# Attention and a low-rank token-mixing MLP in one kernel: another order for the first batch, split fp32r matmuls for t, one PSUM pool

## The chip, the cores and the metric

The kernel runs on one core of one Trainium2 chip. The metric is device time in microseconds (us). The kernel before takes 1001.5 us, the median of three runs (1000.41 to 1001.79). One further execution was recorded by the profiler, and every row of the profile comes from that one.

## The reference

For each of 8 batches, 8 heads, 576 tokens and 64 values per head (q, k and v are inputs in float32):

```python
scores = (q @ k.T) / sqrt(64)
mask_plain = (rel >= 0) & (rel < 32)                       # heads 0 to 3; rel = query position - key position
mask_dil = (rel >= 0) & (rel < 128) & (rel % 4 == 0)       # heads 4 to 7
scores = where(mask, scores, -1e9); scores -= scores.max(-1)
attn = exp(scores); attn /= attn.sum(-1) + 1e-9
x = (attn @ v) as [batch, token, 512]
h = x.T @ U @ V              # per batch, U is [576, 32], V is [32, 576]
u = x + h.T
out = u + relu(u @ w1) @ w2  # w1 is [512, 2048], w2 is [2048, 512]
```

Below, t = Uᵀx is the [32, 512] product of a batch, and the mix is Vᵀt, which is added to x.

## The kernel before

**Precision.** The large matmuls run in fp32r, a form of float32 that keeps fewer bits. To keep the precision, an operand is split into a high part (an fp32r copy) and a low part (what the copy lost), and a product is the sum of three matmuls: high by high, low by high, high by low. A plain fp32 matmul is one instruction in the program and, in the profile, about four times as long as an fp32r one of the same columns (five of 256 columns take 2.51 us, four fp32r ones 0.48 us).

**Attention.** A batch's 18 token tiles of 64 (nine plain, nine dilated) make nine *groups* of two tiles and four units. Groups 0 to 8 are batch 0, 9 to 17 batch 1, and so on to 71. A group's work is: `scores` (32 matmuls, L305), `soft_add` (mask, VectorE, L316), `soft_top` (row maximum, VectorE, L324), the subtraction and exp (GpSimd and ScalarE, L334; from group 9 on four exps on ScalarE, L336), the turn of p into `pts` (TensorE for groups 0 to 17, L342; from group 18 on 16 transposes on VectorE, L358), two steps later `products` (L376), then `weighted` (sums and reciprocal on VectorE, L389 and L390, and the normalisation into x, L416; for groups 0 to 5 the normalisation is eight scaled copies on ScalarE). The dilated half is written to DRAM rows (L428) and fetched back in token order (L433).

**Batch 0** is a loop of its own, steps s = 0 to 10: scores(s), turn_pe(s - 1), products(s - 2), and at the end of a step what lists by engine (`todo`) and the load list name for it: V's unpacking and copies (`pick_v`, L614, which copies V into the four bands of 32 partitions of `vs`), U's unpacking, t of batch 0 (`t_first`, L466), x laid out transposed in PSUM (`lay_x`) with the mix added by matmul (`lay_mix`) and split (`split_sums`, L532), and the unpacking of the first weight pieces (`PRE` gives piece and step). Weights come from DRAM as words that ScalarE, VectorE and GpSimd unpack into high and low parts, one piece for each hidden block and layer (L183, L187, L247).

**The MLP** takes the 36 tiles of 128 tokens in chunks: chunk 0 has four tiles, chunk 1 two, and ten chunks have three. A chunk has 16 hidden blocks, each with twelve first-layer matmuls (ph, L838), the hidden activation hh on ScalarE (L843), its low part hl on VectorE (L844), and for each tile three second-layer matmuls (acc, L857), one hidden block behind.

**The order of the rest.** Instructions stand in each engine's queue in the order in which the program writes them; no scheduler moves them. Between the matmuls of the MLP the program calls `slot()`, seven times a hidden block in chunk 0, five times in chunk 1 and six times later. A queue of side work is sorted by number, and each slot takes out what is due. `STEP_AT` gives the slots of the groups' bursts (`burst`: products of group g - 2 and scores of g); all other numbers follow from these: `split_x` (x into high and low, ScalarE L448 and GpSimd L449), `t_mm` (t by matmul, L476 for batch 1 in fp32, L481 from batch 2 on in fp32r), `t_evict` (t out of PSUM: ScalarE copies, L492, a subtraction on VectorE), `mix` (L501) and `mix_add` (onto x, VectorE, L507), and the transposes that lay out the next chunk (L586 splits them).

**PSUM** has eight banks. Batch 0 uses a pool "first" (ph 2, ps 3, acc 3). Then come a pool with ps 2 and ph 2 and beside it four acc banks in chunk 0, and three acc banks and one mixing bank ("ms", for t and the mix) from chunk 1 on. Closing a pool makes the next one's users wait for the last users of the closed one.

## Time and profile before

| | |
|---|---|
| median of three runs | 1001.5 us |
| profiled execution | 1001.12 us, of which the span is 999.3 us |
| TensorE (PE) busy | 952.0 us |
| VectorE (DVE) busy | 593.6 us |
| ScalarE (ACT) busy | 289.9 us |
| GpSimd (POOL) busy | 89.3 us |
| first weight matmul | at 47.03 us |
| granted clock of TensorE | 0.991 in the mean |

The page names engines PE, PEld (TensorE's weight loads), DVE, ACT, POOL and SP (the queue that issues most DMAs). L838 is line 838 of the kernel. A group's row reads: line, engine, operation, output <- inputs, shapes, count, then busy time and mean duration in ns, then the engine's idle time before it and what ended it. "fp32r" marks an engine's output; the profile writes fp32r operands of matmuls as f32.

### The profile page before, as it was taken

The page shows a single profiled execution, that of the slowest core. Times are in us where ns is not written, and L with a number is a line of the kernel's source. Part 1 is how long each engine was busy: PE and PEld are TensorE (multiplying, and loading weights), DVE is VectorE, ACT ScalarE, POOL GpSimd, SP SyncE. Part 2 cuts the span into 40 slices and gives each one's busy share as a digit, 9 for nine tenths or more (in the row PEclk, how much of TensorE's full clock was granted, in tenths as well). Part 3 has the DMA queues.
Part 4 walks back from the last instruction along what each step waited for, and adds up shares of the span by engine and source line. Part 5 has one row for each costly group of instructions (what it writes and reads, how often), then busy time and mean ns, then how long its engine had stood idle before and what let it go on. Part 6 is the DMA issues. An engine that isn't in the chain of part 4 may idle for free.

```text
span 999.3 us, 22345 instructions
## 1 busy us (share of the span) xinstructions
PE 952.0 (95%) x9000; PEld 812.1 (81%) x9000; DVE 593.6 (59%) x1942; ACT 289.9 (29%) x772; POOL 89.3 (9%) x114
## 2 busy tenths in 40 slices
PE   6799989998999899999899999999999999999998
PEld 4577757787888778888788888888788888999997
DVE  4478776776678667667656766765766753211211
ACT  4577852222222222122222222222321311111110
POOL 3122221000100110010000110010100100000000
PEclk9999998999999999999999999999999999999999
DMA  7467841352143223232323312323214201201000
GB/s 261 165 221 241 258 127 43 90 161 67 48 129 110 65 68 100 87 97 64 106 66 105 102 50 77 109 80 102 79 41 136 81 15 28 66 22 43 32 1 32
DMA packets 79144, 94.30 MB, mean 94 GB/s; under 512 B 8256, under 2 KB 57536, under 8 KB 79040
## 3 DMA queue, kind: packets, MB, share of 16 engines
q1 hardware_dynamic: 79040, 92.86, 30.0%
q8 instruction: 71, 1.16, 0.5%
q14 instruction: 33, 0.27, 0.1%
HBM read 70.81 MB, written 22.02 MB: 93 GB/s over the span
## 4 chain that ended last, share of the span: by engine, by line
PE 70%; DVE 12%; issue 7%; ACT 6%; DMA 2%; SPq 1%; POOL 1%; POOLq 0%; ACTq 0%; DVEq 0%
PE ph L838 32%; PE acc L857 29%; DVE pt L358 2%; PE att L305 2%; PE att L376 2%; ACT hh L843 1%; ACT p L336 1%; DVE vw L187 1%; PE m L501 1%; DVE x L866 1%; PE t L481 1%; POOL xhl L449 1%; DVE hl L844 1%; DVE sign L183 1%; DVE x L416 1%
## 5 line engine op out<-in xcount | busy, mean ns | idle before, releaser
L844 DVE SCALAR_TENSOR_TENSOR hl<-ph,hh 128x384 fp32r<-128x384 f32 (+2 forms) x192 | 106.9, 557 | 302.2 <-ACT hh L843 301.1
L857 PE MATMUL acc<-w2h,hh 128*128 128x512 f32 x576 | 230.5, 400 | 0.0
L857 PE MATMUL acc<-w2h,hl 128*128 128x512 f32 x576 | 227.9, 396 | 1.5 <-DVE hl L844 1.4
L857 PE MATMUL acc<-w2l,hh 128*128 128x512 f32 x576 | 227.6, 395 | 0.9 <-POOL w2l L247 0.9
L843 ACT ACTIVATE hh<-ph 128x384 fp32r<-128x384 f32 (+2 forms) x192 | 93.9, 489 | 463.4 <-PE ph L838 461.8
L358 DVE STREAM_TRANSPOSE pt<-p 32x64 f32<-32x64 f32 x864 | 203.8, 236 | 28.4 <-ACT p L336 14.8
L838 PE MATMUL ph<-uth,w1h 128*128 128x384 f32 (+2 forms) x768 | 168.3, 341 | 3.5 <-ACT uth L586 2.2
L838 PE MATMUL ph<-uth,w1l 128*128 128x384 f32 (+2 forms) x768 | 168.0, 341 | 0.0
L838 PE MATMUL ph<-utl,w1h 128*128 128x384 f32 (+2 forms) x768 | 167.8, 340 | 0.0
L838 PEld LDWEIGHTS ph<-uth,w1h 128*128 128x128 f32 x768 | 136.4, 189 | 20.1 <-ACT uth L586 3.1
L838 PEld LDWEIGHTS ph<-uth,w1l 128*128 128x128 f32 x768 | 133.5, 189 | 4.3 <-issue 0.6
L838 PEld LDWEIGHTS ph<-utl,w1h 128*128 128x128 f32 x768 | 133.4, 189 | 3.7
L857 PEld LDWEIGHTS acc<-w2h,hl 128*128 128x128 f32 x576 | 108.3, 188 | 27.9 <-DVE hl L844 2.6
L857 PEld LDWEIGHTS acc<-w2h,hh 128*128 128x128 f32 x576 | 108.7, 189 | 19.3 <-issue 0.8
L857 PEld LDWEIGHTS acc<-w2l,hh 128*128 128x128 f32 x576 | 108.7, 189 | 17.1 <-POOL w2l L247 1.2
L336 ACT ACTIVATE p<-p,top 128x64 f32<-128x64 f32 x252 | 69.0, 338 | 156.8 <-DVE top L324 156.6
L449 POOL TENSOR_TENSOR xhl<-x,xhl 128x256 fp32r<-128x256 f32 (+1 forms) x60 | 44.7, 755 | 609.9 <-ACT xhl L448 356.2
L305 PE MATMUL att<-qk 64*32 64x64 f32 x2304 | 43.9, 238 | 6.4 <-DMA qk<-qk 5.7
L305 PEld LDWEIGHTS att<-qk 64*32 64x32 f32 x2304 | 35.0, 111 | 11.3 <-DMA qk<-qk 6.2
L316 DVE SCALAR_TENSOR_TENSOR p<-att,mask_sb 128x128 f32<-128x128 f32 x144 | 34.4, 279 | 13.2 <-PE att L305 13.0
L376 PEld LDWEIGHTS att<-v,pt 64*32 64x32 f32 x2016 | 18.8, 106 | 17.6 <-issue 14.0
L501 PE MATMUL m<-ts,vs 128*128 128x256 f32 x66 | 21.2, 321 | 12.3 <-ACT ts L492 7.1
(95 smaller groups left out, 622.8 us busy)
## 6 DMA issues: line engine op xcount, KB each, us to landing
qk<-qk SPq DMA_DIRECT2D x64, 288.0 KB, 3.5
v<-vv SPq DMA_DIRECT2D x126, 130.0 KB, 3.3
...
```

What stands on the lines that cost most here:

```text
L183: nc.vector.scalar_tensor_tensor(out=s32[:, cs], in0=lo, scalar=29, in1=s32[:, cs], op0=ALU.logical_shift_right, op1=ALU.bitwise_or)
L305: nc.tensor.matmul(att[h][r * WIN:(r + 1) * WIN, u * KB:(u + 1) * KB], lhsT=q_, rhs=k_, start=True, stop=True, tile_position=(h * D, r * WIN))
L316: nc.vector.scalar_tensor_tensor(out=p_sb[:, h], in0=att[h][:, 0:2 * KB].rearrange("p (u k) -> p u k", k=KB), scalar=1.0 / 8.0, in1=m, op0 ...
L336: nc.scalar.activation(out=p4[:, n], in_=p4[:, n], func=AF.Exp, bias=top[:, n:n + 1])
L358: nc.vector.transpose(out=pts[g % 2][ks, :, rs], in_=p_sb[rs, :, u, WIN * k:WIN * (k + 1)])
L376: nc.tensor.matmul(att[u][row:row + WIN, o:o + DV], lhsT=pt[us_, h, WIN * r:WIN * (r + 1)], rhs=loaded[g, 1][r // 2][us_, r % 2, h * DV:(h ...
L449: nc.gpsimd.tensor_tensor(out=xhl[rs, 1], in0=x[rs], in1=xhl[rs, 0].bitcast(F32), op=ALU.subtract)
L501: nc.tensor.matmul(mixed[b, i, c], lhsT=vs[:, o:o + P], rhs=t_sb[b, c], start=True, stop=True)
L838: nc.tensor.matmul(ph, lhsT=w[:, k, :], rhs=u[:, k, :], start=(n == 0 and m == 0), stop=(n == 2 and m == KC - 1))
L843: nc.scalar.activation(out=hh, in_=ph, func=AF.Relu)
L844: nc.vector.scalar_tensor_tensor(out=hl, in0=ph, scalar=0.0, in1=hh.bitcast(F32), op0=ALU.max, op1=ALU.subtract)
L857: nc.tensor.matmul(acc[i], lhsT=h[:, ss], rhs=w, start=(c > 1 and f == 1 and n == 0), stop=(f == FC and n == 2))
```

## The change

Nine edits come together.

1. `STEP_AT`: groups 17 and 18 have their bursts at slots 81 and 114 (before, groups 19 and 20 at 95 and 114). The products of groups 16 and 17 have bursts of their own (`LAST`, slots 90.6 and 94.1), without scores.
2. One PSUM pool for the whole program: ps 2, ph 2, acc 4. t from batch 2 on and the mix use the acc banks.
3. Batch 0: all loads are issued first, the first weight piece behind them, and the first two pieces are unpacked in other steps (`PRE`).
4. V's four copies are made by eight split fp32r matmuls in steps 6 and 7 (before: four fp32 matmuls in step 3), through ph banks, with the picking matrices and V split beforehand.
5. t of batch 0 is made by split fp32r matmuls from x split on ScalarE and GpSimd (`split_first`), but for the one part `t_first(3, 0)`, which stays fp32. t of batch 1 is made as in later batches, by `split_x` and two fp32r matmuls a part.
6. U's stationary matrix has 128 columns for each part: three copies of the high part and the low part. So t comes out of PSUM in four bands.
7. `t_evict` is one ScalarE copy of 128 partitions and one VectorE subtraction on 32 of them (before: a copy, a subtraction and one or two further copies).
8. The normalisation of groups 0 to 5 moves from ScalarE to VectorE.
9. The high and the low halves of `split_sums` are issued apart; t starts five slots behind the splits (before four, or nine behind the first); the mix comes four slots behind the eviction's number.

```diff
-PRE = [(0, 6), (1, 10)]
+PRE = [(0, 8), (1, 9)]
-NX = 17
+NX = 16
-STEP_AT = [(NGB, 2), (2 * NGB + 1, 95), (2 * NGB + 2, 114), (3 * NGB + 1, 232), (4 * NGB + 1, 342), (NG + 1, 914)]
+STEP_AT = [(NGB, 2), (2 * NGB - 1, 81), (2 * NGB, 114), (3 * NGB + 1, 232), (4 * NGB + 1, 342), (NG + 1, 914)]
...
-    first = first_open.enter_context(tc.tile_pool(name="first", bufs=3, space=bass.MemoryType.PSUM))
+    psum = ctx.enter_context(tc.tile_pool(name="psum", bufs=2, space=bass.MemoryType.PSUM))
-    us = const.tile([P, 9, 2 * RANK], F32R, name="us")
+    us = const.tile([P, 9, 4, RANK], F32R, name="us")
...
-                if g < 6:
+                if g < 0:
                     for h in range(2):
                         nc.scalar.activation(out=o[:, h], in_=pv[rs, h, 0:D], func=AF.Copy, scale=ssum[rs, u, h:h + 1])
...
+        pool, tag, n_ = (work, "z", ZS) if b == 1 and i < 2 else (xpool, "x", NX)
+        xhl = pool.tile([P, 2, HALF_D], F32R, tag=tag, name=f"xhl{b}_{i}_{c}", bufs=n_)
...
+    def split_first(i, c):
...
+        nc.scalar.copy(out=xhl[rs, 0], in_=m[rs])
+        xs[0, i, c] = xhl
+        rest[i, c] = lambda: nc.gpsimd.tensor_tensor(out=xhl[rs, 1], in0=m[rs], in1=xhl[rs, 0].bitcast(F32), op=ALU.subtract)
...
     def t_first(i, c):
...
-        nc.tensor.matmul(t_ps[0, c], lhsT=u32[rs, k * RANK:(k + 2) * RANK], rhs=m[rs],
-                         start=new, stop=(i == (0 if c else len(DPART) - 2)), skip_group_check=True)
+        xhl = xs.pop((0, i, c))
+        for k in range(2):
+            nc.tensor.matmul(t_ps[0, c], lhsT=u, rhs=xhl[:, k], start=(new and k == 0), stop=(last and k == 1),
+                             skip_group_check=True)
...
     def t_evict(b, c):
-        nc.scalar.copy(out=ts_[r[0]], in_=tp[r[0]])
-        nc.vector.tensor_tensor(out=ts_[r[1]], in0=tp[r[0]], in1=ts_[r[0]].bitcast(F32), op=ALU.subtract)
-        if b > 0:
-            nc.scalar.copy(out=ts_[r[2]], in_=tp[r[1]])
-        nc.scalar.copy(out=ts_[r[3]], in_=tp[r[0]])
+        nc.scalar.copy(out=ts_, in_=tp)
+        nc.vector.tensor_tensor(out=ts_[lo], in0=tp[lo], in1=ts_[lo].bitcast(F32), op=ALU.subtract)
...
-        mixed[b, i, c] = accs.tile([P, HALF_D], F32, tag="ms", name=f"m{b}_{i}_{c}", bufs=1)
+        mixed[b, i, c] = psum.tile([P, HALF_D], F32, tag="acc", name=f"m{b}_{i}_{c}", bufs=4)
...
-    loads = {0: [lambda: load_qk(5), lambda: load_v(4)], 1: [lambda: load_qk(6), lambda: load_v(5)],
-             2: [lambda: load_qk(7), lambda: load_v(6)], 3: [lambda: load_qk(8), lambda: load_v(7), lambda: w_fetch(0)],
-             4: [lambda: load_v(8), lambda: w_fetch(1)], 5: [lambda: w_fetch(2)], 6: [lambda: w_fetch(3)],
...
+    for g in range(4, NGB):
+        load_qk(g)
+        load_v(g - 1)
+    load_v(NGB - 1)
+    w_fetch(0)
+    loads = {3: [lambda: w_fetch(1)], 5: [lambda: w_fetch(2)], 7: [lambda: w_fetch(3)], 8: [lambda: w_fetch(4)],
...
+    def pick_v(i):
+        vps[i] = psum.tile([P, 2, VC], F32, tag="ph", name=f"vps{i}", bufs=2)
+        for k in range(2):
+            for m in range(2):
+                nc.tensor.matmul(vps[i][:, k], lhsT=picks[:, m, 2 * i + k].rearrange("p i r -> p (i r)"), rhs=vhl[:, m],
+                                 start=(k == 0 and m == 0), stop=(k == 1 and m == 1), skip_group_check=True)
+    def keep_v(i):
+        nc.scalar.copy(out=vs[:, 2 * i * VC:2 * (i + 1) * VC], in_=vps.pop(i).rearrange("p k c -> p (k c)"))
...
+    LAST = [step_at(2 * NGB - 1) + 9.6, step_at(2 * NGB - 1) + 13.1]
+    for i, at_ in enumerate(LAST):
+        g = 2 * NGB - LAG + i
+        add(step_at(2 * NGB - 1) + 1 + i, take_v, g)
+        add(at_, burst, -1, g)
+        add(at_ + 1, after_burst, -1, g)
...
-            at_ = max([end_1 if c == 0 else 0] + splits) + (5 if c == 0 else 9)
             if b == 1:
-                at_ = step_at(2 * NGB + c * -1 + 1) + 3
+                at_i = [LAST[0] - 4 + 1.2 * i for i in range(n)] if c else [LAST[0] + 2.5 + 0.6 * i for i in range(n - 2)] + [LAST[1] + 1.5, LAST[1] + 2]
+                at_t = [LAST[1] + 2.5 + 0.3 * i for i in range(n)] if c else [LAST[1] + 4.5 + 0.3 * i for i in range(n)]
+            else:
+                at_i = [splits[i] + i if c else max(splits[0:i + 1] + [end_1]) + 0.02 * i for i in range(n)]
+                at_t = [a + 5 for a in at_i]
+            at_ = at_t[-1] + 0.3
+            m_at = FIRST + 4 + 12 * (1 - c) if b == 1 else at_ + 4
```

Three places show how the order moves. The first is the queue of SP in batch 0, from the values of group 5 to the first weight piece (raw0). qk and v are a group's loads, xd0 the rows of the dilated half that are written to DRAM. Before:

```order
L282 DMA v5_187<-vv 128x520
L428 DMA xd0_246<-xp0_241 128x256
L270 DMA qk7_250<-qk 128x576
L282 DMA v6_252<-vv 128x520
L428 DMA xd0_246<-xp1_316 128x256
L270 DMA qk8_322<-qk 128x576
L282 DMA v7_324<-vv 128x520
L221 DMA raw0_326<-w1 128x4x256
```

With the change:

```order
L280 DMA v5_131<-vv 128x520
L268 DMA qk7_133<-qk 128x576
L280 DMA v6_135<-vv 128x520
L268 DMA qk8_137<-qk 128x576
L280 DMA v7_139<-vv 128x520
L280 DMA v8_141<-vv 128x520
L219 DMA raw0_143<-w1 128x4x256
L425 DMA xd0_254<-xp0_251 128x256
```

All loads of batch 0 and the first weight piece now stand ahead of the first write of dilated rows.

The second is TensorE at the end of batch 1, in hidden block 14 of chunk 0 (t1_0 and t1_1 are the two halves of t of batch 1, att the banks of scores and products). Before:

```order
L305 MATMUL att19_1_2074<-qk19_1757 32x64 x4
L838 MATMUL ph0_14_2107<-uth0_698,w1h_13_1876 128x512 x4
L838 MATMUL ph0_14_2107<-uth0_698,w1l_13_1877 128x512 x4
L838 MATMUL ph0_14_2107<-utl0_699,w1h_13_1876 128x512 x4
L476 MATMUL t1_0_2150<-x4_506,us_73 64x256
L476 MATMUL t1_0_2150<-x5_1591,us_73 64x256
L476 MATMUL t1_0_2150<-x6_1593,us_73 64x256
L476 MATMUL t1_0_2150<-x7_1595,us_73 64x256
L476 MATMUL t1_0_2150<-x8_1561,us_73 64x256
L857 MATMUL acc0_0_800<-w2h_13_1878,hh0_13_2020 128x512
```

With the change:

```order
L494 MATMUL t1_1_2106<-xhl1_0_1_1940,us_73 128x256 x2
L494 MATMUL t1_1_2106<-xhl1_1_1_1952,us_73 128x256 x2
L872 MATMUL ph0_14_2083<-utl0_756,w1h_13_1892 128x512 x4
L494 MATMUL t1_1_2106<-xhl1_2_1_1968,us_73 128x256 x2
L494 MATMUL t1_1_2106<-xhl1_3_1_1990,us_73 128x256 x2
L494 MATMUL t1_1_2106<-xhl1_4_1_2016,us_73 128x256 x2
L891 MATMUL acc0_0_822<-w2h_13_1894,hh0_13_1986 128x512
L891 MATMUL acc0_0_822<-w2l_13_1895,hh0_13_1986 128x512
L891 MATMUL acc0_0_822<-w2h_13_1894,hl0_13_1987 128x512
L494 MATMUL t1_0_2136<-xhl1_0_0_2043,us_73 128x256 x2
L494 MATMUL t1_0_2136<-xhl1_1_0_2047,us_73 128x256 x2
```

The scores of group 19 are no longer there, both halves of t stand between the pieces of the MLP, and each part is two matmuls on a split of x.

The third is VectorE at the same place, around the normalisation of group 17, the last of batch 1 (ssum17, x7 and x8; vw and sign are a weight piece's unpacking, p18 and p19 belong to groups 18 and 19 of batch 2). Before:

```order
L358 STREAM_TRANSPOSE pt0_79<-p18_1966 32x2x32 x2
L187 SCALAR_TENSOR_TENSOR vw29_2033<-vw29_2033,sign1_76 128x512
L358 STREAM_TRANSPOSE pt0_79<-p18_1966 32x2x32 x2
L389 TENSOR_SCALAR ssum17_2114<-att19_0_2073 128x2
L389 TENSOR_SCALAR ssum17_2114<-att19_1_2074 128x2
L390 RECIPROCAL ssum17_2114<-ssum17_2114 128x4
L416 TENSOR_TENSOR x7_1595<-att19_0_2073,ssum17_2114 64x128
L416 TENSOR_TENSOR x7_1595<-att19_1_2074,ssum17_2114 64x128
L416 TENSOR_TENSOR x8_1561<-att19_0_2073,ssum17_2114 64x128
L416 TENSOR_TENSOR x8_1561<-att19_1_2074,ssum17_2114 64x128
L316 SCALAR_TENSOR_TENSOR p19_2122<-att19_0_2073,mask_sb_71 128x128
```

With the change:

```order
L181 SCALAR_TENSOR_TENSOR sign1_76<-raw29_0_1978,sign1_76 128x256
L181 SCALAR_TENSOR_TENSOR sign1_76<-raw29_1_1979,sign1_76 128x256
L185 SCALAR_TENSOR_TENSOR vw29_2027<-vw29_2027,sign1_76 128x512
L386 TENSOR_SCALAR ssum17_2088<-att17_0_2056 128x2
L386 TENSOR_SCALAR ssum17_2088<-att17_1_2057 128x2
L387 RECIPROCAL ssum17_2088<-ssum17_2088 128x4
L413 TENSOR_TENSOR x7_1644<-att17_0_2056,ssum17_2088 64x128
L413 TENSOR_TENSOR x7_1644<-att17_1_2057,ssum17_2088 64x128
L413 TENSOR_TENSOR x8_1615<-att17_0_2056,ssum17_2088 64x128
L413 TENSOR_TENSOR x8_1615<-att17_1_2057,ssum17_2088 64x128
```

The transposes of group 18 and the mask of group 19 no longer stand around the normalisation.

249 lines of the change are left out of this document (125 added, 124 removed).

## The prediction

> **What bounds the kernel now.** I read the page first, then TensorE's waits in three stretches, then the order of time around the two places where they gather. The page:
>
> ```profile
> span 999.3 us, 22345 instructions
> PE 952.0 (95%) x9000; PEld 812.1 (81%) x9000; DVE 593.6 (59%) x1942; ACT 289.9 (29%) x772; POOL 89.3 (9%) x114
> ```
>
> TensorE is busy for 952 of 999.3 us, so an edit counts where TensorE idles, runs slowly or does work it need not do. The idle 47 us lie in three places. The first is the attention of batch 0, before the first weight matmul (columns: start, duration, instructions, idle time before and what ended it):
>
> ```profile
> 10.37 0.68 PE L305 MATMUL att<-qk 64*32 64x64 f32 x32 [0.18 <-DMA qk<-qk]
> 12.12 2.69 PE L614 MATMUL vps<-vn,pick 128*128 128x176 f32 x8
> 18.81 0.68 PE L305 MATMUL att<-qk 64*32 64x64 f32 x32
> 20.63 0.68 PE L305 MATMUL att<-qk 64*32 64x64 f32 x32
> 28.06 0.69 PE L342 MATMUL ptp<-id_sb,p 128*128 128x128 f32 x2 [2.05 <-ACT p L334]
> 28.68 1.97 PE L466 MATMUL t<-xp,u 128*64 128x256 f32 x4
> 33.98 0.46 PE L376 MATMUL pv<-v,pt 64*32 64x65 f32 x32
> 35.35 1.08 PE L466 MATMUL t<-x,u 128*64 128x256 f32 x4 [0.53 <-ACT t L492]
> 47.03 2.01 PE L838 MATMUL ph<-uth,w1h 128*128 128x512 f32 x4 [1.24 <-DVE utl L532]
> 20.33 6.07 DMA raw<-w
> ```
>
> The L305 rows are the scores of groups 3, 5 and 6; an undisturbed step takes 20.63 - 18.81 = 1.82 us. From group 3's scores to step 9 (33.98) are six steps and 23.6 us. What stretches them is V's copies (2.69 us), the t matmuls (1.97 us for two calls), and the exp behind the last row, which is of the chain of waits: ScalarE had the first weight piece, still in flight, ahead of the exp in its queue.
>
> The second place is the end of batch 1 (window rows: stretch, length, busy time of PE, PEld, DVE, ACT and POOL, granted clock, DMA):
>
> ```profile
> 135.37 2.51 PE L476 MATMUL t<-x,us 64*64 64x256 f32 x10
> 149.83 4.68 PE L476 MATMUL t<-x,us 64*64 64x256 f32 x10 [3.32 <-DVE p L316]
> 148.49 1.00 DVE L416 TENSOR_TENSOR x<-att,ssum 64x128 f32<-64x128 f32 x4
> 148.00:150.00 2.00, 0.17 (x1) 0.20 (x2) 1.86 (x10) 0.18 (x1) 0.00 (x0) 0.88 0.02 5
> 150.00:152.00 2.00, 2.00 (x5) 0.83 (x5) 1.49 (x6) 1.10 (x4) 0.00 (x0) 0.50 0.00 0
> 156.00:158.00 2.00, 2.00 (x10) 1.59 (x9) 0.83 (x3) 1.98 (x6) 1.15 (x1) 0.91 0.00 0
> ```
>
> TensorE idles 3.32 us because VectorE, full in that stretch, normalises the last group of batch 1 only at 148.49; then the clock is granted at half for about 6 us (three such rows from 150 to 156, the first shown), and the same ten t instructions take 4.68 us instead of 2.51.
>
> The third place is the short waits in batches 2 to 7 (TensorE's waits, window 250 to the end: total, times, longest):
>
> ```profile
> PE m L501 <- ACT ts L492: 6.0, 4, 2.8
> PE t L481 <- POOL xhl L449: 3.4, 8, 0.5
> PE t L481 <- ACT xhl L448: 3.0, 4, 1.3
> PE m L501 <- DVE x L507: 2.9, 6, 1.3
> ```
>
> **The change, part by part.** (a) The prelude. As many bytes as before lie ahead of group 3's keys, so its scores stay near 10.4. The weight piece is now fetched behind all of batch 0 but used only in step 8, so the wait for it goes, and V's copies leave step 3. The normalisation of groups 0 to 5 moves from ScalarE to VectorE, which I take as what paces the steps (groups of VectorE, 10 to 34 us; the L416 row from 170 to 226):
>
> ```profile
> L324 DVE TENSOR_REDUCE top<-p 128x4 f32<-128x256 f32 x7 | 2.9, 420 | 0.7
> L316 DVE SCALAR_TENSOR_TENSOR p<-att,mask_sb 128x128 f32<-128x128 f32 x12 | 2.9, 282 | 5.1 <-PE att L305 5.0
> L389 DVE TENSOR_SCALAR ssum<-pv 128x2 f32<-128x2 f32 x14 | 1.5, 149 | 0.0
> L390 DVE RECIPROCAL ssum<-ssum 128x4 f32<-128x4 f32 x7 | 1.2, 177 | 0.2
> L183 DVE SCALAR_TENSOR_TENSOR sign<-rawu,sign 128x448 int32<-128x448 int32 x1 | 1.0, 1002 | 0.0
> L187 DVE SCALAR_TENSOR_TENSOR u<-u,sign 128x448 int32<-128x448 int32 x1 | 0.6, 625 | 0.0
> L416 DVE TENSOR_TENSOR xp<-att,ssum 128x128 f32<-128x128 f32 (+1 forms) x10 | 2.4, 286 | 0.2
> ```
>
> One step: 2 x 0.282 + 0.420 + 2 x 0.149 + 0.177 + 2 x 0.286 = 2.0 us. Six steps are 12.2; U's unpacking adds 1.6, V's about 0.7 (176 columns of 448, with a floor), group 4's second half 0.6: 15.1. In TensorE's queue between one step's turn and the next scores now stand V's eight split matmuls and six t passes. From 1.97 us for two fp32 calls of four passes each a pass of 256 columns costs 0.25 at that speed: 1.5 for t, 1.4 for V, and up to 1 us until ScalarE has copied V out of the one bank that the second half and t0 share. Half of this lies beside VectorE's work; I charge 1.5. Step 9 comes at 10.4 + 16.6 = 27.0 instead of 34.0: 7 us. Behind step 9 stood 13.0 us; the wait of 1.24 us for all subtractions should mostly go with the pool's closing, but GpSimd now has five to seven subtractions in series ahead of the last t. I credit 0.5. Sum (a): 7.5 us, between 3 and 10.
>
> (b) The end of batch 1. Ten fp32 t calls become 20 passes; two rows show the pace of 256 columns at full clock:
>
> ```profile
> 199.37 0.64 PE L838 MATMUL ph<-uth,w1h 128*128 128x256 f32 x4
> 199.85 0.64 PE L838 MATMUL ph<-uth,w1l 128*128 128x256 f32 x4
> ```
>
> Four take 0.48 us, so 20 take 2.4, against 2.51 + 4.68/2 = 4.85 at full clock: 2.4 saved. The last products now come without scores, in slots 90.6 and 94.1, and group 18's scores only in slot 114, so the transposes of groups 18 and 19 no longer stand ahead of the normalisation on VectorE. If the idle 3.32 us goes, so does the half clock (0.12 x 2 + 0.5 x 6 + 0.09 x 2 = 3.4 us lost). Together 9.1. New there are ten splits:
>
> ```profile
> L449 POOL TENSOR_TENSOR xhl<-x,xhl 128x256 fp32r<-128x256 f32 x48 | 35.6, 755 | 358.9 <-ACT xhl L448 277.8 <-issue 23.4 <-PE ph L838 19.2
> L448 ACT CAST xhl<-x x60: 387/402/409, 220.2 to 828.3; 128x256 fp32r<-128x256 f32 x48, 64x256 fp32r<-64x256 f32 x12
> 120.00:146.00 26.00, 24.93 (x286) 18.17 (x285) 20.28 (x54) 18.50 (x52) 6.59 (x5) 1.00 0.51 158
> L336 ACT ACTIVATE p<-p,top 128x64 f32<-128x64 f32 x12 | 3.5, 337 | 8.2 <-DVE top L324 8.2
> ```
>
> ScalarE (18.5 of 26 us busy) gets 10 x 0.40 = 4.0 us and loses the eight exps of groups 18 and 19 (2.7 us) and four of six t copies; GpSimd (6.6 of 26) gets 7.6 us. Is the last split in time? Count from T, the end of the 14th ph, by estimates from the rows. TensorE has two product bursts (1.0), seven second-layer blocks of three (7 x 0.7 = 4.9, by 2.08 us for nine, quoted in (c)), one ph (2.8) and seven t parts (1.7) ahead of it: T + 10. On the other side ScalarE runs one hidden activation, two splits and a piece's four copies (7 x 0.4 = 2.8), VectorE unpacks and normalises (2.6), ScalarE copies (two pieces' rest and two splits, 1.6), GpSimd subtracts twice (1.5): T + 8.5. Behind it in ScalarE's queue stand the hidden activations, behind those the second layer. I charge 1.1. Sum (b): 8, between 2 and 9.
>
> (c) Batches 2 to 7. In the program's count a three-tile chunk has six slots per hidden block, and these rows of the chain of waits give the slot's length:
>
> ```profile
> 247.52 2.10 PE ph L838 x12
> 260.08 2.08 PE acc L857 x9
> ```
>
> (2.10 + 2.08)/6 = 0.70 us. Split to t grows from four slots to five, against waits of 0.5 us (GpSimd) and at most 1.3 (ScalarE): of 6.4 us I leave 2.0, with 0.5 in it because batch 2's five splits now fall together. The eviction loses two copies and their queueing behind VectorE, and the mix moves a slot away: of 6.0 I leave 2.0. The 2.9 for the one mixing bank stay. That is 8.4; since waits move when everything before them moves, I take 7, between 3 and 10.
>
> (d) The price. By the program's numbers groups 18 to 28 come every 118/10 = 11.8 slots instead of 118/8 = 14.75 (from group 20 on), most of them in chunk 1:
>
> ```profile
> 170.00:226.00 56.00, 53.77 (x691) 47.19 (x690) 42.72 (x163) 12.32 (x40) 2.18 (x3) 1.00 0.44 131
> L358 DVE STREAM_TRANSPOSE pt<-p 32x64 f32<-32x64 f32 x87 | 20.5, 236 | 1.4
> PE m L501 <- DVE x L507: 2.2, 3, 1.5
> ```
>
> 1.3 more groups in chunk 1, each 16 x 0.236 + 2.0 = 5.8 us, raise VectorE from 42.7 to about 50 of 56 us (90%). Against some 2 us of late hl stand the 2.2 us of mixing waits (the last row, window 47 to 250), which fall away since chunk 1 holds two of the four acc banks. Net 0, between -4 and +2. Keeping one PSUM pool costs no instruction; t's wider stationary side (128 columns instead of 64) costs nothing, since the ph rows above hold their pace with 128.
>
> Sum: 7.5 + 8 + 7 + 0 = 22.5 us. The profiled execution took 1001.12 us, 0.4 below the median of the runs and 1.8 above its span: 978.6, with the median 979.
>
> **The rivals.** *The prelude stays slow.* TensorE's batch 0 speed doubled only within its dense stretch (two t calls: 1.97 us at 28.68, 1.08 at 35.35). The change thins that stretch. If the array is still slow for the 32 fp32 instructions that lay x out, then at about 0.125 us more each (2.50 us for 20 fast ones) 4 us go and (a) is 3.5: 983. Against it: those instructions are dense themselves. The Trainium skill, "TensorE: Matmul & The Clock Gate", Part 1, says that the array runs at half clock by default, goes to full after about 3.4 us of sustained activity and falls back after an idle window of that length; the fall after 3.32 us idle agrees. By that rule it is this rival that the thinner prelude gets, with 983. The window rows of the prelude grant 1.00 throughout, so there only durations can tell.
>
> *The wait at the end of batch 1 comes back in another form.* ScalarE's queue holds weight unpacking, splits and hidden activations in one order; if it is 3 us behind, TensorE waits for GpSimd's last split and the clock falls again: (b) keeps the 2.4 us of passes and little else: 985.
>
> *The waits of batches 2 to 7 only move.* (c) gives 0 to 1: 985.5.
>
> *Slower.* VectorE at 90% in chunk 1 cannot keep the step of 11.8 slots; a group's transposes finish later than its products, TensorE waits 3 us and falls to half clock. One such gap costs 3.3 + 3.4 = 6.7 us by the rows at 148 to 158. It decides from the fourth gap in chunk 1 and the first third of chunk 2: 978.6 + 26.8 = 1005. For it speaks the in-order queue; against it that two steps lie between scores and products, and that VectorE at 42.7 of 56 us made TensorE idle only 2.2 us.
>
> **How the numbers follow.** Forecast 0.56 (own range 972 to 984), slow prelude 0.14 (983), returned wait 0.13 (985), moved waits 0.12 (985.5), slower 0.03 (1005); 0.02 for a mix that ends level. Two of the middle rivals together give 990. The upper ends of (a) to (d) give 31 us and 970. The range is 969 to 991. Under 0.2% (2 us) cannot be told from no change; faster by more: 0.95, same 0.02, slower 0.03.
>
> **What would show it.** The first weight matmul should start between 37 and 41 us, not 47.0 (slow prelude: 42 to 44, with lay-out matmuls at 0.25 us). The half clock near 150 should be gone and t of batch 1 should take about 2.4 us of TensorE in all. The sum of the four waits from 250 on should be 6 to 9 us instead of 15.3. VectorE should show about 90% in chunk 1 with hl as a wait of under 3 us. A first weight matmul after 44, or a half clock anywhere behind 60 us, would make the prediction wrong.

## The result and the profile after

The changed kernel takes 982.78 us, the median of four runs (982.27 to 982.89), against 1000.95 us for the kernel before in the same session. The ratio is 0.982, 95% interval 0.9803 to 0.9837: faster by 18 us. The forecast was 979, with a range of 969 to 991. The page of its profiled execution (982.7 us) begins:

```profile
span 980.8 us, 22338 instructions
PE 942.0 (96%) x9000; PEld 815.3 (83%) x9000; DVE 600.0 (61%) x1953; ACT 281.1 (29%) x735; POOL 109.3 (11%) x139
```

TensorE is busy 10 us less and idle 8.5 us less. To see where, both spans are cut at the same places of the program: where the hidden activation of the first block starts (end of the prelude), of the 17th (start of chunk 1), of the 49th (start of chunk 3) and of the 192nd, the last. Window rows of the kernel before (stretch, length, busy time of PE, PEld, DVE, ACT, POOL, granted clock, DMA share, GB/s):

```profile
0.00:52.56 52.56, 38.42 (x717) 25.50 (x718) 24.68 (x83) 26.77 (x77) 11.60 (x22) 0.97 0.62 208
52.56:173.44 120.88, 114.38 (x1131) 86.62 (x1130) 89.81 (x218) 77.40 (x186) 27.10 (x20) 0.97 0.56 179
173.44:312.11 138.67, 131.73 (x1436) 114.43 (x1435) 100.15 (x370) 35.02 (x106) 8.83 (x13) 1.00 0.32 95
312.11:991.30 679.19, 663.31 (x5705) 582.58 (x5704) 376.35 (x1269) 150.24 (x403) 41.77 (x59) 0.99 0.23 70
```

And of the changed kernel:

```profile
0.00:46.02 46.02, 35.10 (x718) 27.49 (x719) 26.54 (x94) 24.68 (x59) 21.02 (x35) 1.00 0.71 238
46.02:162.50 116.48, 107.51 (x1034) 84.12 (x1033) 84.53 (x183) 77.74 (x185) 37.67 (x32) 1.00 0.56 180
162.50:305.49 142.99, 135.81 (x1532) 117.42 (x1531) 109.24 (x404) 35.38 (x110) 8.75 (x13) 0.99 0.32 98
305.49:972.81 667.32, 659.44 (x5705) 583.26 (x5704) 377.08 (x1269) 142.85 (x384) 41.84 (x59) 1.00 0.24 71
```

| stage | before | after | difference |
|---|---|---|---|
| prelude | 52.56 | 46.02 | -6.5 |
| chunk 0 | 120.88 | 116.48 | -4.4 |
| chunks 1 and 2 | 138.67 | 142.99 | +4.3 |
| chunks 3 to 11 | 679.19 | 667.32 | -11.9 |

So the rework around the end of batch 1 gains 4.4 us in chunk 0 and gives 4.3 back in chunks 1 and 2; the gain comes from the prelude and from the late batches. Some work has moved too: two bursts of scores and one of products now fall into chunks 1 and 2 instead of chunk 0. With the TensorE time that one of each takes to itself in chunks 0 to 2 (11.6 us for 23 bursts of scores, 7.0 for 22 of products) that is about 1.3 us; what is left is 3.1 won and 3.0 lost. These are two single traces. The changed kernel and eight runs below have the same instructions in chunks 0 to 2, but for the slots and copies of t of batch 2 in four of them, and take 258.1 to 259.8 us for these chunks (259.5 in the changed kernel, 259.6 in the kernel before). So a difference of less than 2 us in these chunks is not to be read from one trace.

**Prelude** (order of time, TensorE):

```profile
20.13 0.47 PE L302 MATMUL att<-qk 64*32 64x64 f32 x16 [1.94 <-issue]
26.14 1.24 PE L484 MATMUL t<-xhl,ud 128*128 128x256 f32 x4 [0.84 <-ACT vs L642]
29.89 0.90 PE L373 MATMUL pv<-v,pt 64*32 64x65 f32 x32 [0.31 <-ACT pt L345]
32.40 2.76 PE L526 MATMUL tp<-id_sb,x 128*128 128x128 f32 x12
38.47 0.72 PE L484 MATMUL t<-xhl,us 128*128 128x256 f32 x4
41.48 1.51 PE L872 MATMUL ph<-uth,w1h 128*128 128x512 f32 x4
```

The products of step 9 come at 29.89 (33.98 before), the first weight matmul at 41.48 (47.03). The last us of the 6.5 lies in the twelve matmuls behind it: before, they fell into a stretch of half clock (47.12 to 50.54).

**End of batch 1:**

```profile
135.62 0.68 PE L373 MATMUL att<-v,pt 64*32 64x65 f32 x32 [1.37 <-issue]
139.57 0.71 PE L494 MATMUL t<-xhl,us 128*128 128x256 f32 x4 [1.21 <-DVE x L413]
143.53 0.50 PE L891 MATMUL acc<-w2l,hh 128*128 128x512 f32 x1 [1.39 <-POOL w2l L245]
```

The idle 3.32 us is not gone. It has become three waits, 3.97 us in all: for nothing that the profile shows, for the normalisation on VectorE, and for a weight's low part on GpSimd, which now stands behind the splits. What is gone is the half clock: the row of chunk 0 grants 1.00.

**Chunk 1.** TensorE's row near 216 us, ScalarE's and VectorE's behind it:

```profile
214.94 0.42 DVE L321 TENSOR_REDUCE top<-p 128x4 f32<-128x256 f32 x1
215.40 1.06 ACT L333 ACTIVATE p<-p,top 128x64 f32<-128x64 f32 x4 [5.42 <-DVE top L321]
216.37 0.36 ACT L877 ACTIVATE hh<-ph 128x256 fp32r<-128x256 f32 x1
216.78 0.79 PE L891 MATMUL acc<-w2h,hh 128*128 128x512 f32 x1 [2.08 <-ACT hh L877]
216.73:220.14 3.41, 3.36 (x8) 0.50 0.46 134
```

VectorE reaches the row maximum of a group only at 214.94. The exps wait for it, the hidden activation stands behind the exps on ScalarE, and TensorE waits 2.08 us for that; the next 3.41 us have half clock.

**Batches 2 to 7** (TensorE's waits from 250 on):

```profile
PE m L511 <- DVE x L517: 3.9, 7, 1.6
PE t L494 <- POOL xhl L447: 3.4, 9, 0.4
PE t L494 <- ACT xhl L446: 1.1, 3, 0.5
```

The four waits that the prediction summed to 15.3 us are 8.4 (3.9 + 3.4 + 1.1; the wait of the mix for the eviction, 6.0 us, is gone). That is 7 us of the 8.0 us by which TensorE's idle time falls there; 3.4 more are two stretches of half clock that the kernel before had, at 340.67 and 562.54 (window rows of the kernel before, each stretch with the one ahead of it):

```profile
337.25:340.67 3.42, 0.75 (x4) 1.00 0.21 66
340.67:344.08 3.41, 3.29 (x11) 0.50 0.00 0
559.12:562.54 3.42, 1.65 (x10) 1.00 0.45 152
562.54:565.95 3.41, 3.41 (x12) 0.50 0.02 5
```

### The profile page after: what moved, and what is told of

Same layout as the page of the kernel before. It is cut to its first block, busy times and chain, and to the rows that moved or that the text cites. A ratio compares the mean times of both kernels' runs of the same rounds, so it can differ in the third digit from the quotient of the medians.

```text
span 980.8 us, 22338 instructions
## 1 busy us (share of the span) xinstructions
PE 942.0 (96%) x9000; PEld 815.3 (83%) x9000; DVE 600.0 (61%) x1953; ACT 281.1 (29%) x735; POOL 109.3 (11%) x139
## 4 chain that ended last, share of the span: by engine, by line
PE 72%; DVE 9%; issue 9%; ACT 5%; POOL 3%; DMA 2%; SPq 1%; POOLq 0%; ACTq 0%; DVEq 0%
PE ph L872 33%; PE acc L891 31%; PE att L302 2%; POOL xhl L447 2%; DVE pt L355 2%; PE att L373 2%; ACT p L333 1%; PE t L494 1%; ACT hh L877 1%; DMA qk<-qk 1%; DVE vw L185 1%; PE m L511 1%; DMA v<-vv 1%; DVE top L321 1%; DVE p L313 1%
## 5 line engine op out<-in xcount | busy, mean ns | idle before, releaser
L447 POOL TENSOR_TENSOR xhl<-x,xhl 128x256 fp32r<-128x256 f32 (+1 forms) x70 | 52.5, 762 | 606.5 <-ACT xhl L446 426.9
L446 ACT CAST xhl<-x 128x256 fp32r<-128x256 f32 (+1 forms) x70 | 26.6, 401 | 27.6 <-DVE x L413 14.8
```

Of the source, the lines that this page charges most:

```text
L446: nc.scalar.copy(out=xhl[rs, 0], in_=x[rs])
L447: nc.gpsimd.tensor_tensor(out=xhl[rs, 1], in0=x[rs], in1=xhl[rs, 0].bitcast(F32), op=ALU.subtract)
```

## The experiments

All are the changed kernel with the edit shown, and all are set against the kernel before of the same session by their ratio (the changed kernel itself: 0.982, 0.9803 to 0.9837). What compares stages uses the same four cuts as above.

### The prelude: loads, normalisation, t

Loads spread over the steps:

```diff
-    for g in range(4, NGB):
-        load_qk(g)
-        load_v(g - 1)
-    load_v(NGB - 1)
-    w_fetch(0)
-    loads = {3: [lambda: w_fetch(1)], 5: [lambda: w_fetch(2)], 7: ...
+    load_qk(4)
+    load_v(3)
+    loads = {0: [lambda: load_qk(5), lambda: load_v(4)], 1: [lambda: load_qk(6), lambda: load_v(5)],
+             2: [lambda: load_qk(7), lambda: load_v(6)], 3: [lambda: load_qk(8), lambda: load_v(7), lambda: w_fetch(0)],
+             4: [lambda: load_v(8), lambda: w_fetch(1)], 5: [lambda: w_fetch(2)], 7: ...
```

> The changed kernel with one part undone: batch 0's loads are spread over the steps again (keys of group 5 in step 0, and so on, the first weight piece in step 3). Everything else stays. Theory of the prediction: the order of the loads as such is worth nothing, because the weight piece is used late in any case; the first weight matmul stays at 41.5 us within 0.5 and the time within 1 us of 982.8. Theory of the trace after: the loads issued all at once hold up TensorE's own supply of instructions, which shows as two idle stretches put down to issue (1.13 us before 14.10 and 1.94 us before 20.13); then these shrink to less than 1 us in all and the first weight matmul comes 1 to 3 us earlier, time 980 to 982. Third: keys or weights now come too late; the first weight matmul comes after 42.5 and the time is above 984.

Measured: 983.01 us, ratio 0.982 (0.9793 to 0.9847); first weight matmul at 42.42; TensorE's waits for "issue" 3.6 us in three places (3.1 in two in the changed kernel). These waits did not shrink, so the theory that the loads cause them falls, and the time stayed, as the prediction's theory had it. What causes them is open. In ten traces whose prelude has the same instructions (the changed kernel and nine runs below) the first weight matmul comes between 39.7 and 42.2, 40.8 in the mean. The waits for "issue" largely go with it: 0.8 us in the traces with 39.80 and 39.98, 3.4 us in the one with 42.16. So they vary from one execution to the next though the instructions are the same, and 42.4 is late by little more than this scatter: the order of the loads is worth 0 to 2 us.

Normalisation of groups 0 to 5 on ScalarE:

```diff
-                if g < 0:
+                if g < 6:
```

> The changed kernel with one part undone: the normalisation of groups 0 to 5 is on ScalarE again (28 scaled copies of about 0.23 us, 6.4 us in all, by the trace of before). Theory that ScalarE's queue was what stretched the steps: the exp and the turned copies stand behind these copies, the steps are 0.5 to 0.9 us longer, the first weight matmul comes 2 to 4 us later, time 985 to 987. Theory that VectorE paces the steps, as the prediction has it (2.0 us a step with the normalisation in it, 1.4 without): the first weight matmul comes up to 2 us earlier, time 981 to 983.

Measured: 984.92 us, 0.9837 (0.981 to 0.9864); first weight matmul at 44.33, 2.2 us later than the latest of those ten and 3.5 later than their mean. TensorE's waits for the copies in this run, and the wait for the exps in the kernel before (0 to 47 us):

```profile
PE pv L373 <- ACT xp L411: 1.7, 2, 0.8
PE pv L373 <- ACT x L411: 1.3, 1, 1.3
PE ptp L342 <- ACT p L334: 4.3, 4, 2.1
```

TensorE's products wait 3.0 us for these copies. They wait for no normalisation in the changed kernel, where it is on VectorE, so VectorE has room for the work. But they wait for none in the kernel before either, which has the same copies on ScalarE: there the products shared three ps and three acc banks with the scores, and in the one pool they have two ps banks, so a late copy holds up the next products. What TensorE waited for there were the exps, 4.3 us; that wait is gone in the changed kernel (0.2) and stays gone in this run, so the copies by themselves do not hold the exps up. So 3.5 us is what the copies on ScalarE would cost in the new pool. What the move was worth against the kernel before, and which of the other edits took the exps' wait away, no run parts. This is the one part of the prelude's edits whose worth stands clear of the scatter in the trace; the times alone do not part it from the changed kernel.

t of batch 0 in plain fp32:

```diff
-        xhl = xs.pop((0, i, c))
-        for k in range(2):
-            nc.tensor.matmul(t_ps[0, c], lhsT=u, rhs=xhl[:, k], ...
+        m = x_tile(t)[:, 0:HALF_D] if c == 0 else xps.pop(i)
+        rs = slice(row, row + n) if c == 0 else slice(0, P)
+        nc.tensor.matmul(t_ps[0, c], lhsT=u.bitcast(F32)[rs], rhs=m[rs], start=new, stop=last, skip_group_check=True)
...
-        todo["act"].append((s, both(split_first, i, c)))
-        todo["pool"].append((s + (s < 10), lambda i=i, c=c: rest[i, c]()))
```

> The changed kernel with one part undone: t of batch 0 is made by plain fp32 matmuls from x itself, nine splits on ScalarE and GpSimd fall away (3.5 us and 6.9 us of those engines). V's copies stay split. Theory that TensorE's passes are on the path of the prelude: 9 parts take two passes more each, 18 passes of 0.12 to 0.25 us, first weight matmul 2 to 4.5 us later (43.5 to 46), time 985 to 987. Theory that the chain of splits paces the end of the prelude: the first weight matmul stays or comes earlier (40 to 42), time 981 to 983.

Measured: 982.25 us, 0.9817 (0.9785 to 0.9849); first weight matmul at 41.02, as the second theory had it. Splitting x for batch 0 gains nothing that stands clear of the scatter: the passes saved on TensorE and the splits on ScalarE and GpSimd cancel, or both lie beside other work.

### Batch 1: the passes, the bursts, or both

t of batch 1 in plain fp32, in the same slots:

```diff
+        if b == 1:
+            rs = slice(row, row + n)
+            nc.tensor.matmul(t_ps[b, c], lhsT=us[:, u_of(n, tok)]....bitcast(F32)[rs],
+                             rhs=x_tile(t)[rs, c * HALF_D:(c + 1) * HALF_D], start=at_first, stop=at_last)
+            return
...
-                add(at_i[i], split_x, b, i, c)
+                if b > 1:
+                    add(at_i[i], split_x, b, i, c)
```

> The changed kernel with one part undone: t of batch 1 is made by plain fp32 matmuls in the same slots, ten splits fall away (4.0 us of ScalarE, 7.6 us of GpSimd). Theory of the prediction: 20 passes of 0.12 us more, so 2.4 us later at the end of chunk 0, less the wait for the low half of the weights (1.39 us before 143.53) that the splits on GpSimd cause: net 1 us, time 983 to 985. Rival: without splits nothing is to be waited for and the three waits at 134 to 144 us (4.0 us) go with them: time 981 to 982. Second rival: the waits gather in one stretch, TensorE is granted half clock again for 3.4 us or more, time 986 or above.

Measured: 980.91 us, 0.9802 (0.9775 to 0.9829). Of the 4.0 us of waits between 134 and 144 us 1.2 are left, both put down to "issue"; those for x and for the weight's low part are gone, as the rival said. What that is worth is small: chunks 0 to 2 take 258.9 us, within the 258.1 to 259.8 of the traces with the splits, and the intervals of the two ratios overlap. Half clock fell once in these chunks, at 109 us. Of those nine traces four have half clock there too (from 107.7 to 110.9 us on), and their chunk 0 takes 117.4 to 117.5 us; here it takes 116.4. So by these traces the waits that the splits cause cost about 1 us more than the passes that they save.

The whole of batch 1 as before:

```diff
-STEP_AT = [(NGB, 2), (2 * NGB - 1, 81), (2 * NGB, 114), ...
+STEP_AT = [(NGB, 2), (2 * NGB + 1, 95), (2 * NGB + 2, 114), ...
...
-    for i, at_ in enumerate(LAST):
-        ...
-        add(at_, burst, -1, g)
...
-        p_ = g - LAG if g >= 2 * NGB + LAG or NGB + LAG <= g < 2 * NGB else -1
+        p_ = g - LAG if g >= NGB + LAG else -1
...
+                at_t = [step_at(2 * NGB + 1 - c) + 3 + 0.01 * i for i in range(n)]
```

> The changed kernel with the whole rework of batch 1 undone: bursts of groups 19 and 20 at slots 95 and 114, products and scores in one burst, t of batch 1 by plain fp32 matmuls. The prelude, the one PSUM pool, the eviction and the times from batch 2 on stay as changed. Theory of the prediction (terms b and d): this costs 8 us, time 989 to 993. Theory of the two traces laid side by side: from the first to the 48th hidden activation of the program (chunks 0 to 2) both kernels take the same time (259.55 us before, 259.47 us after), because what the end of batch 1 gains is lost in chunks 1 and 2; then the time is 981 to 985, the half clock is back near 145 us, and the one near 217 us is gone.

Measured: 978.61 us, 0.9779 (0.9755 to 0.9802): undoing the rework makes the kernel faster. The windows of chunk 0 and of chunks 1 and 2, and TensorE's long wait:

```profile
46.27:165.67 119.40, 111.68 (x1130) 87.39 (x1129) 90.42 (x218) 75.92 (x183) 27.06 (x20) 0.99 0.56 181
165.67:302.13 136.46, 132.38 (x1436) 116.81 (x1435) 99.85 (x370) 33.87 (x102) 8.80 (x13) 0.99 0.32 97
143.53 0.67 PE L494 MATMUL t<-x,us 64*128 64x256 f32 x2 [3.68 <-DVE p L313]
```

Together 255.9 us against 259.5: 3.6 us less, with the wait of 3.68 us and two stretches of half clock (at 145.14 and 220.23) in it. That is 2.2 us below the lowest of the nine traces with the rework. TensorE idles 11.8 us in chunks 0 to 2, 16.1 in the changed kernel. Since plain fp32 t on the new bursts takes 258.9, it is the bursts, not the split, that cost 3 of these us. The expectation had read the two traces as equal up to chunk 2 and was still too kind: the kernel before takes 259.6 us for these chunks, so the other edits gain some 3.7 us there. Which of them was not followed.

Batch 1's bursts as before, but t split, in later slots:

```diff
+                at_i = [80 + 0.8 * i for i in range(n)] if c else [max(a, 90.5 + 0.6 * i) for i, a in enumerate(splits)]
+                at_t = [step_at(2 * NGB) + 3 + 0.3 * i for i in range(n)] if c else [step_at(2 * NGB + 1) + 7 + 0.3 * i for i in range(n)]
```

> The kernel with batch 1's bursts as before (groups 19 and 20 at slots 95 and 114, products and scores together), but t of batch 1 by split fp32r matmuls, the second half seven slots behind the burst of group 19 instead of three. Theory that on the old schedule it is the wait for the last x that costs, and that a later slot removes it: against the kernel with the whole of batch 1 as before, 978.6 us, the idle 3.68 us at 139.85, the half clock behind it (1.7 us) and 20 passes (2.2 us) go, less 1 to 2 us of new waits: 971 to 975. Rival: the splits on ScalarE and GpSimd hold weights and hidden activations up, as the waits at 134 to 144 us in the changed kernel did: 977 to 980.

Measured: 981.61 us, 0.9807 (0.9786 to 0.9828); chunks 0 to 2 take 261.1 us. Both theories missed:

```profile
137.79 0.43 ACT L176 ACTIVATE vw<-raw 128x256 f32<-128x256 f32 x1 [3.15 <-DMA raw<-w]
140.57 0.35 ACT L501 CAST ts<-t 128x256 fp32r<-128x256 f32 x1
141.90 0.40 PE L373 MATMUL att<-v,pt 64*32 64x65 f32 x20 [4.77 <-DVE ts L502]
```

The wait moved ahead. ScalarE stands 3.15 us at a weight piece still in flight; the eviction of t's first half is queued behind it; the burst of group 19 needs the bank that t holds; TensorE idles 4.77 us. Why the weight came late was not followed. The profiled execution is also the slowest of the four (984.8, the others 980.9 to 982.3), so the wait may be shorter in the others.

### The pace of groups 18 to 28

```diff
-STEP_AT = [(NGB, 2), (2 * NGB - 1, 81), (2 * NGB, 114), ...
+STEP_AT = [(NGB, 2), (2 * NGB - 1, 81), (2 * NGB, 107), ...
...
-                first = step_at(NGB * b + ODD + LAG) + (9 if b == 1 else 12)
+                first = max(step_at(NGB * b + ODD + LAG) + (9 if b == 1 else 12), 196.8 if b == 2 else 0)
```

> The changed kernel with one number changed: group 18's burst in slot 107 instead of 114, so that groups 18 to 28 come every 12.5 slots instead of 11.8 (the first half of batch 2's splits is held where it was). Theory that the pace of 11.8 slots is too fast for VectorE in chunk 1 and so exps and hidden activations on ScalarE come late: the waits of the second layer for hh near 190 and 215 us (0.69 and 2.08 us) and the half clock that can follow them go, time 978 to 981. Rival: the waits have another cause, time 982 to 984.

Measured: 978.77 us, 0.9769 (0.9752 to 0.9786), clear of the changed kernel's interval: this is the fastest of the versions by its ratio, level with the whole of batch 1 as before. The two waits for hh, 2.8 us, have become one of 0.5; TensorE's idle time in chunk 1 falls from 4.1 to 0.7 us. The profiled execution shows less of it (chunks 0 to 2: 258.5 us): it is the slowest of the four, 981.12 against 977.7 to 979.4, and half clock fell twice there (108.94 and 224.99) and once in the changed kernel. So the slots of these bursts made the hidden activations late. That the pace was too fast for VectorE as such is not shown: it works 47.2 us in chunk 1 here and 48.4 in the changed kernel, and here the chunk is 4.5 us shorter. The edit also starts the row of bursts seven slots earlier, and no run parts the start from the pace.

### Batches 2 to 7: the copies, the slots, the pool

Three copies of 32 partitions in the eviction, as before:

```diff
-        nc.scalar.copy(out=ts_, in_=tp)
-        nc.vector.tensor_tensor(out=ts_[lo], in0=tp[lo], in1=ts_[lo].bitcast(F32), op=ALU.subtract)
+        if b < 2:
...
+        else:
+            nc.scalar.copy(out=ts_[r[0]], in_=tp[r[0]])
+            nc.vector.tensor_tensor(out=ts_[r[1]], in0=tp[r[0]], in1=ts_[r[0]].bitcast(F32), op=ALU.subtract)
+            nc.scalar.copy(out=ts_[r[2]], in_=tp[r[2]])
+            nc.scalar.copy(out=ts_[r[3]], in_=tp[r[3]])
```

> The changed kernel with one part undone: from batch 2 on t leaves PSUM by three ScalarE copies of 32 partitions and a VectorE subtraction between them, as before. Theory of the prediction (term c, 4.0 us of it from eviction and the slot of the mix): the waits of the mix for the eviction come back, 2 to 4 us in all, and with them possibly one half clock of 3.4 us: time 984 to 988. Rival: the later slot of the mix alone hides it: 982 to 983.5.

Measured: 982.2 us, 0.982 (0.9799 to 0.9842); chunks 3 to 11 take 668.5 us (667.3): 1 us. The rival held: the mix waits 0.2 us for the eviction.

t four slots behind the split, the mix three behind the eviction:

```diff
-                at_t = [a + 5 for a in at_i]
+                at_t = [a + 4 for a in at_i]
...
-            m_at = ... else at_ + 4
+            m_at = ... else at_ + 3
```

> The changed kernel with one part undone: from batch 2 on t comes four slots behind the split and the mix three behind the eviction, as before (after: five and four). Theory of the prediction (term c, 4.4 us of it from the slot of t): waits of t for the splits of 3 to 6 us come back, time 985 to 989, more where a stretch of half clock falls in. Rival: the slots are not what mattered, the copies of the eviction were: 982 to 983.5.

Measured: 983.0 us, 0.9825 (0.9799 to 0.9851); chunks 3 to 11 take 670.5 us: 3.2 us. The waits of t for the splits are 6.3 us instead of 4.9, but the mix waits less for VectorE's additions (1.3 us instead of 3.9), and TensorE idles 7.9 us there in both. So the 3.2 us are two stretches of half clock. One, behind the longest of the waits for a split (544.58), belongs to the slot; a second one (698.18) follows a window with 1.21 us of idle time, which is not understood. The words "as before" in this expectation are not exact: in the kernel before, the eviction came 1.5 slots behind the last t and the mix 2.5 behind the eviction. The next two runs part these.

Both edits together:

```diff
-        nc.scalar.copy(out=ts_, in_=tp)
+            nc.scalar.copy(out=ts_[r[0]], in_=tp[r[0]])
...
-                at_t = [a + 5 for a in at_i]
+                at_t = [a + 4 for a in at_i]
...
-            m_at = ... else at_ + 4
+            m_at = ... else at_ + 3
```

> The changed kernel with the long eviction and the slots of before (t four behind the split, mix three behind the eviction) undone together, so that of the change from batch 2 on only the PSUM pool stays (t and the mix in the acc banks, no mixing bank of their own). Each of the two alone brought at most 1 us of waits back. Theory that either is enough: the mix finds t in time if it comes a slot later or if the eviction is short; with both undone the 6.0 us of waits of the mix for the eviction come back, with half clocks 988 to 992. Theory that the pool did it: the time stays at 981 to 985 and no wait of the mix for the eviction is above 1 us.

Measured: 982.57 us, 0.9808 (0.9793 to 0.9824); chunks 3 to 11 take 670.3 us. The waits of the mix for the eviction are 0.5 us in all. The first theory falls. By the second it would be the pool, but one number of before is still missing here: the eviction's.

The eviction's number as before too (the edit against the run just before):

```diff
-            at_ = at_t[-1] + 0.3
+            at_ = at_t[-1] + 0.3 if b == 1 else max([end_1 if c == 0 else 0] + splits) + (5 if c == 0 else 9) + 0.5
...
-            m_at = ... else at_ + 3
+            m_at = ... else at_ + 2.5
```

> As the run with the long eviction and the earlier slots, but with the numbers of before to the half slot: from batch 2 on t four slots behind the split, the eviction 1.5 slots behind the last t, the mix 2.5 slots behind the eviction (that run had the eviction 0.3 behind the last t and the mix 3 behind the eviction, the changed kernel 0.3 and 4). Of the change from batch 2 on only the PSUM pool and the wider t stay. Theory that the slots made the gain of 11.9 us behind chunk 2: the mix again waits for the eviction 4 to 6 us in all, the longest wait near 335 us is above 2 us, time 986 to 992. Theory that the pool made it: these waits stay below 1 us in all and the time at 981 to 985.

Measured: 993.42 us, 0.9932 (0.9915 to 0.995). The last stage and TensorE's wait from 250 on:

```profile
303.60:983.22 679.62, 663.92 (x5705) 585.83 (x5704) 376.29 (x1269) 150.10 (x403) 41.74 (x59) 0.99 0.23 70
PE m L517 <- ACT ts L508: 6.1, 4, 2.8
```

679.6 us against the 679.2 of the kernel before: the whole gain of 11.9 us is gone, with the one PSUM pool still in place. So the pool by itself gains nothing there, and the slots, with the copies, are worth all of it. Of the 9.3 us by which this run is longer there than the one before it 7.2 are idle time of TensorE and 1.7 one more stretch of half clock. How, the eviction near 330 us shows (ScalarE, VectorE, TensorE):

```profile
327.89 0.35 ACT L505 CAST ts<-t 32x256 fp32r<-32x256 f32 x1
329.60 1.01 DVE L413 TENSOR_TENSOR x<-att,ssum 64x128 f32<-64x128 f32 x4
331.04 0.41 DVE L506 TENSOR_TENSOR ts<-t,ts 32x256 fp32r<-32x256 f32 x1
332.28 0.58 PE L517 MATMUL m<-ts,vs 128*128 128x256 f32 x1 [2.78 <-ACT ts L508]
```

The same place in the kernel before:

```profile
336.40 0.35 ACT L488 CAST ts<-t 32x256 fp32r<-32x256 f32 x1
338.11 1.01 DVE L416 TENSOR_TENSOR x<-att,ssum 64x128 f32<-64x128 f32 x4
339.55 0.41 DVE L489 TENSOR_TENSOR ts<-t,ts 32x256 fp32r<-32x256 f32 x1
340.79 0.58 PE L501 MATMUL m<-ts,vs 128*128 128x256 f32 x1 [2.78 <-ACT ts L492]
```

In the run with both edits but the eviction 0.3 slots behind the last t:

```profile
325.50 0.41 DVE L506 TENSOR_TENSOR ts<-t,ts 32x256 fp32r<-32x256 f32 x1 [1.13 <-ACT ts L505]
```

And in the changed kernel:

```profile
330.28 0.42 DVE L502 TENSOR_TENSOR ts<-t,ts 32x256 fp32r<-32x256 f32 x1
331.20 1.01 DVE L413 TENSOR_TENSOR x<-att,ssum 64x128 f32<-64x128 f32 x4
331.41 0.28 PE L511 MATMUL m<-ts,vs 128*128 128x256 f32 x1
```

With the late number the subtraction stands behind a group's normalisation and mask on VectorE and comes 2.8 us after the first copy (331.04 - (327.89 + 0.35); in the kernel before 339.55 - (336.40 + 0.35) = 2.8 too); the other copies wait for it, and the mix for them. With the early number it stands ahead of the normalisation, and the mix waits for nothing. The mix itself is even nearer to t there (3.3 slots, 4.0 in the other): it is the eviction's place in VectorE's queue that decides. Both runs have the long eviction; whether the short one at the late number would wait as long was not run.

### What makes the clock fall

Waits of chosen lengths in the last two chunks, where TensorE otherwise never idles; the rest of the work is unchanged, so the kernel is longer by them:

```diff
+    def gap(name, n):
+        g0 = psum.tile([P, HALF_D], F32, tag="ps", name=f"gap{name}", bufs=2)
+        nc.tensor.matmul(g0[:, 0:P], lhsT=id_sb, rhs=id_sb, start=True, stop=True)
+        sb = work.tile([P, 2, P], F32, tag="p", name=f"hold{name}", bufs=2)
+        nc.scalar.copy(out=sb[:, 0], in_=g0[:, 0:P])
+        for i in range(n):
+            nc.scalar.copy(out=sb[:, 1], in_=sb[:, 0])
+        nc.tensor.matmul(g0[:, P:2 * P], lhsT=sb[:, 1 if n else 0], rhs=id_sb, start=True, stop=True)
```

> The changed kernel with 14 waits put into its last two chunks, where TensorE otherwise never idles: a small matmul, ScalarE copies it out and copies on 0 to 6 times, and a second small matmul waits for the last copy. The waits should be 0.9 to 3.0 us long. Theory of the traces so far: TensorE's clock is decided by a fixed grid of 3.413 us (the starts of all stretches of half clock of one run are whole multiples of it apart), and a piece of the grid in which TensorE idles more than half (1.71 us; 1.68 did not do it, 1.77 did) is followed by a piece at half clock. Then waits below 1.7 us never lead to half clock, waits of 1.7 to 3.4 us do where one piece of the grid holds 1.71 us of them, and a wait that the grid divides does not. Rival: it goes by the length of one wait: all above about 2 us lead to it, wherever they lie. Second rival: only a wait of some 3.4 us does, then none of these.

Measured: 1018.13 us. A wait of 2.49 us and one of 1.83, and the windows around them (the grid is taken from the starts of the half-clock stretches):

```profile
892.96 0.49 PE L858 MATMUL gap<-id_sb,hold 128*128 128x128 f32 x2 [2.49 <-ACT hold L857]
887.94:891.35 3.41, 2.52 (x15) 1.00 0.00 0
891.35:894.76 3.41, 1.80 (x9) 1.00 0.29 77
911.83:915.24 3.41, 1.58 (x10) 1.00 0.00 0
915.24:918.66 3.42, 3.42 (x11) 0.50 0.00 0
```

The wait of 2.49 us is divided by the grid (0.89 and 1.61 idle) and no half clock follows; the one of 1.83 lies in one window, and it does. Of the 14 waits four led to half clock: both of 1.83, one of 2.16 and the other of 2.49, each with 1.83 us or more in one window. The other waits of 2.16 and 2.49 us, which the grid divides, led to none. The theory of the grid held, and both rivals fell.

## Why the prediction was right, and which of its steps were not

The total was forecast at 22.5 us and came out at 18.5 by the profiled spans. The range held it, but two of the four terms were wrong and a third came out far above its size: the errors are -1.0 in (a), -4.9 in (b), -3.0 in (d) and +4.9 in (c). That the total came within 4 us is in part luck.

Of the signs that the prediction set itself, the half clock near 150 is gone, t of batch 1 takes about 2.7 us of TensorE (2.4 foretold) and the four waits are 8.4 us. The first weight matmul, at 41.48, lies a little above the 37 to 41 foretold. But it also said that a half clock anywhere behind 60 us would make it wrong, and there is one at 216.73. So by its own sign the account of the kernel failed though the time came; the step is (d), below.

**(a) Prelude, 7.5 us: right in size (5.6 to the first weight matmul, 6.5 with the half clock behind it), its reason in part open.** The prediction took VectorE as what paces the steps and the moved normalisation as a load on it. TensorE waits for no normalisation on VectorE, and back on ScalarE the copies cost about 3.5 us in the new pool. The wait for the exp behind the weight piece (2.05 us) went as foretold, and with it the others for exps (4.3 us in all, 0.2 after). From group 3's scores (9.82) to step 9 it took 20.1 us, not 16.6: the waits for "issue" (3.1 us) are not in the 2.0 us a step. Behind step 9 it was 11.6 us instead of 13.0, better than the 0.5 credited. The rival of a slow prelude was half true: twelve of the 32 lay-out matmuls took 0.23 us each, the rest about 0.15, and four passes of t took 1.24 us at 26.14 and 0.72 at 38.47. The argument that the window rows grant 1.00 throughout the prelude does not hold: the clock's record begins at 33.47 us in the trace of the kernel before and at 35.82 in that of the changed one, and ahead of it a row reads 1.00 for want of a record. Where it begins earlier it shows the slow stretch. In the run with t of batch 1 in plain fp32 (stretch, length, TensorE's busy time, granted clock, DMA share, GB/s):

```profile
27.11:33.92 6.81, 6.49 (x116) 0.50 0.50 150
```

Four passes of t just ahead of this stretch, at 26.33, took 0.71 us, and four within it, at 30.61, took 1.54.

**(b) End of batch 1, 8 us: wrong; 3.1 us in chunk 0 once the moved bursts are counted.** The passes (about 2 us: t of batches 1 and 2 takes 8.3 us of TensorE to itself in the run with batch 1 as before and 6.1 in the changed kernel) and the half clock (3.4) came as forecast. The step that failed is "I charge 1.1" for what the splits put into ScalarE's and GpSimd's queues, together with counting the idle 3.32 us as gone. Idle time in chunk 0 rose from 6.5 to 9.0 us; without the splits it is 5.7. The rival of a returned wait named the mechanism and the engine (GpSimd), but the wait was a weight's low part behind the splits, not the last split itself.

**(d) VectorE in chunk 1, net 0: wrong; 3.0 us lost in chunks 1 and 2.** VectorE was busy 46.6 us from 170 to 226, less than the 50 of the prediction, and it was still too late twice. The rival "slower" was near to this mechanism at 6.7 us a gap and from the fourth gap on, but with transposes that come too late for the products; here it was a row maximum, and behind it the exps and the hidden activation on ScalarE. There was one such gap, of 2.08 us with one stretch of half clock (1.7 us), and a smaller one. That VectorE made TensorE idle only 2.2 us in the kernel before did not show that it would hold: no hidden activation was late there, and none is listed among TensorE's waits from 173 to 312 us. With group 18's burst seven slots earlier the waits for hh all but go at the same VectorE time, so it is the slots of the bursts and not VectorE's share that the step had to price. With (b), the edit that the forecast valued at 8 us costs 3.6 by the two traces, 4 by the medians: the run with all of batch 1 as before is faster than the change.

**(c) Batches 2 to 7, 7 us: right in kind, 11.9 in size for chunks 3 to 11.** The four waits fell to 8.4 us, within the 6 to 9 foretold. Missed were the two stretches of half clock behind two of those waits (2.78 us for the eviction, 1.77 for a split), worth 3.4 us; the prediction speaks of the clock only near 150 us and in the prelude, and the half clock at 47.12 it missed too. It credited the short eviction and the mix's slot together with 4.0 us, and it had the mechanism, copies that queue behind VectorE. The edit that made the gain, the eviction 0.3 instead of 1.5 slots behind the last t, it does not name: the runs give 9 us to that (679.6 - 670.3, clock included), and 3 us to the copies and the slots of t and the mix together (1 to the copies alone).

The bounds held because one term came out above its upper end while two lay near their lower ends, not because the terms were known. A forecast that (b) and (d) come to nothing and (c) to 12 would have given 982 for better reasons.
